# Four of the eight loads of the middle filter piece issued from GpSimd instead of SyncE

## The chip, the cores and the metric

The kernel runs on one core of a Trainium2 chip. The time is the device time of one execution in microseconds (us). TensorE does the matrix products (PE in the profile, PEld its weight loads), VectorE is DVE, ScalarE is ACT, GpSimd is POOL, SyncE is SP. SP computes nothing here; it issues DMA transfers, each of which the chip's DMA engines then carry out.

## The reference

With x of 2048 x 512 in bf16, two blocks are chained, each on a layer norm and each added to its input:

```
h  = x + irfft2( rfft2( layernorm(x) ) * (w_r + i w_i) )
h2 = h + ( gelu( layernorm(layernorm(h)).T @ w1 + b1 ) @ w2 + b2 ).T
```

The filter w_r, w_i has 2048 rows (frequencies along the sequence) and 257 columns (frequencies along the features); w1 is 2048 x 1376 and w2 is 1376 x 2048.

## The kernel before

**Stages.** The 2-D transform is done as matrix products with constant matrices. Stage A (line 593) transforms along the sequence: 16 row groups `A0` to `A15`, each four products of x with the Fourier matrix `FS`, which GpSimd scales by the rows' reciprocal deviation (`fs0` to `fs15`, line 577). Their results are copied out of PSUM as `Ye` (line 607). Then the spectrum is worked through in 16 chunks c. For each chunk: `Bc` (line 637) transforms along the features, `Bec` copies it out (line 641); `Cc` (line 652, mostly two chunks at once, named `C2p`, `C4p` and so on) finishes the sequence transform, `Cec` copies it out into `Xsb` (line 665); `Pc` (line 674, on DVE) multiplies the chunk by its part of the filter tile `W`; `Ic` (line 692) starts the inverse transform with the product as weights, and `Iec` copies its result into `TT` (lines 708 and 709). After the last chunk the inverse transform along the features (`Bi`, lines 864 and 771) and along the sequence (`Ai`) are done row group by row group, with the second layer norm (`sq`, `A2`, `hh`), and each normed row group `hh` is multiplied by w1 at once (`m1`, line 844). Then come gelu, the products with w2 (`m2`, lines 962 and 968), the final addition (`fin`, line 974) and the stores.

**Order.** Each engine runs a list of operations in a fixed order, written out by hand in `K.schedule` (line 979). What a list leaves out is placed by a small list scheduler with priorities. GpSimd's list holds the sixteen `fs`, then seven small operations `nm` (negated row means, line 617, used from the second layer norm on), three small loads of biases, and three casts of these (lines 937 to 940). SP's list is left to the scheduler: the loads go in order of `prio`. The chunk products stand in DVE's list in the order P0 P1, P3 P2, P4, P5, P7 P6, P9 P8, P10 P11, P13 P12, P14 P15, with copies out of PSUM between them.

**PSUM banks.** `I` of chunk c writes bank 5 + c % 3 (the last half of chunk 15 writes bank 0), so I14 must wait until Ie11 has copied out, and I15 until Ie12 has.

**The filter loads** (lines 510 to 523). `W` is loaded in three pieces of the index tau: 0 to 8, 8 to 18, 18 to 32. Chunk c reads tau 2c and 2c+1, so the middle piece serves P4 to P8, and the last one P9 to P15. A piece has two components, w_r and w_i, and each component four loads (six in the first piece), because a tau has four rows in four partitions. A load of the middle piece carries 32 partitions x 10 rows of 512 bytes, 160 KB; one of the last piece 14 rows, 224 KB. The source rows are 514 bytes apart.

**Waits.** All loads with one `group` share a semaphore, and whoever reads such a tile waits until all loads of the group have landed. `wgroup` only tells the dependency tracker that writes of one piece need no order among themselves. So P4 waits for all of the middle piece, and P9 for all of the last.

**After the filter** SP issues the constants `ID`, `GD` and `IF`, eight loads of w1 and eleven of w2; some of the last wait for buffers of the chunk stage to come free.

Of the kernel before, what the change touches and what calls it, by code (L numbers as in the profile page):

```python
# [11 lines left out]
NP = 128  # L12
# [453 lines left out]
def build_kernel(nc, A_x, A_w_r, A_w_i, B_w1, B_b1, B_w2, B_b2, out, verbose=False):  # L466
# [10 lines left out]
    X, Y, FS, F, E, Lm, Hm, W, TT, GD, IF = (T[n] for n in ("X", "Y", "FS", "F", "E", "Lm", "Hm", "W", "TT", "GD", "IF"))  # L477
# [9 lines left out]
    def dma(name, q, dst, src, nbytes, prio=0.0, after=(), group=None, wgroup=None, store=False, land=None):  # L487
        def emit(e, eng):
            with nc.allow_non_contiguous_dma(reason="layout"):
                return eng.dma_start(dst, src)  # L490
        return K.op(name, q, emit, ins=[src] if store else [], outs=[] if store else [dst], occ=450.0, prio=prio,
                    after=after, nbytes=nbytes, group=group, wgroup=wgroup, land=land)
# [18 lines left out]
    for pi, (ta, tb) in enumerate(pieces):  # L511
        for comp, wsrc in enumerate((A_w_r, A_w_i)):
            wv = wsrc.rearrange("(q r) k -> q r k", r=64)
            for reim in range(2):
                parts = [(0, ta, tb, wv[:, ta:tb, 1:257])]
                lo = ta
                if ta == 0:
                    parts.append((1, 0, 1, wv[:, 32:33, 1:257]))
                    lo = 1
                parts.append((1, lo, tb, wv[:, 64 - lo:64 - tb:-1, 1:257]))  # L520
                for ss, a, b, src in parts:
                    dma(f"ld_w{comp}_{pi}_{reim}_{ss}_{a}", "sp", W[2 * ss + reim:NP:4, a:b, comp, :], src, 32 * 512 * (b - a),
                        prio=1.0 + pi, group=f"W{pi}", wgroup=f"W{pi}")

    K.op("mk_eps", "dve", lambda e, eng: eng.memset(eps[:, 0:1], LN_EPS), outs=[eps[:, 0:1]], occ=70.0, lat=130.0, prio=0)  # L525
    K.op("mk_eps2", "dve", lambda e, eng: eng.memset(eps[:, 1:2], LN_EPS * LN_EPS), outs=[eps[:, 1:2]], occ=70.0, lat=130.0, prio=0)
# [21 lines left out]
    for ga, gb in RS_GROUPS:  # L548
# [18 lines left out]
        for n2 in range(ga, gb):  # L567
            if n2 < NSPLIT:
                for sg in range(2):
# [4 lines left out]
                         prio=-5 + 0.1 * g)  # L574
# [380 lines left out]
    for n2 in range(NS2):  # L955
        b = 3 + n2 % 5
# [14 lines left out]
        else:  # L971
# [19 lines left out]
               "ag14 bn15 ag15 Ye6 Ye10 Ye14 Be2 Ce0 P0 P1 Ie0_0 P3 P2 Be7 P4 Be8 P5 Ie2_0 P7 P6 Ie4_0 P9 P8 Ie6_0 P10 P11 Ie7_0 P13 P12 "  # L991
               "Ie10_0 P14 P15 Ie14_0 Ie15_0 Bie01 bq01 bq00 aq0 sd2_1 sd2_0 hh00 hh01 h01 h00 hh1 h2 sd3_0 sd3_1 sd4_0 sd4_1 h3 sd5_1 hh2 "
               "sd5_0 h4 sd6_1 sd6_0 hh3 h5 sd7_1 hh4 h6 sd8_0 sd7_0 hh5 sd8_1 h7 sd9_1 hh6 sd9_0 h8 hh7 sd10_1 sd10_0 h9 hh8".split(),
        "pool": "fs1 fs0 fs2 fs4 fs5 fs3 fs6 fs7 fs8 fs9 fs12 fs10 fs11 fs13 fs14 fs15 nm2 nm7 nm3 nm4 nm0 nm1 nm8 ld_b1a ld_b2 ld_b1b b2f "
               "b1f_a b1f_b".split(),
    })
    K.gen_sync()
# [31 lines left out]
def bass_sequential_preLN__spectral_gfnet__mixer_token_mlp__prompt_kernel(  # L1029
    nc,  # L1030
    A_x,
    A_w_r,
    A_w_i,
    B_x,
    B_w1,
    B_b1,
    B_w2,
    B_b2,
    out,
):  # L1040
    build_kernel(nc, A_x, A_w_r, A_w_i, B_w1, B_b1, B_w2, B_b2, out)
# [28 lines left out]
```

## Time and profile before

| | us |
|---|---|
| median of 4 runs | 130.95 (130.55 to 131.06) |
| the profiled execution | 130.05 |
| its span, first to last instruction | 128.2 |
| PE busy in the span | 121.2 |
| DVE busy | 65.1 |
| ACT busy | 65.1 |
| POOL busy | 12.3 |

The span is that of the profiled execution; 1.85 us of its time lie outside the span. The granted TensorE clock is 1.00 throughout. Bytes read are 20.49 MB, written 2.10 MB. A timeline line names the start, the time, the engine, the line of the code, the operation, what it writes and reads, and in brackets how long the engine sat idle before it and what released it. "SPq" rows are the issuing of transfers by SP, not the transfers. For the transfers, the profile gives the time from the issue to the landing. All loads and stores have line 490, that of the helper `dma`.

### The profile page before, as it was taken

The numbers are of one execution on the slowest core, as the hardware profiler recorded it, in microseconds if no ns is written. First come the engines' busy times: TensorE is split into PE (matmuls) and PEld (weight loads), VectorE is DVE, ScalarE is ACT, GpSimd is POOL, SyncE is SP. The second block draws the span as 40 slices with busy tenths as digits, with TensorE's granted clock in tenths as the row PEclk, the third lists the DMA queues.
The fourth block names the chain that finished last, engine by engine and source line by source line (L and its number), as shares of the span: only waits on it lengthen the run. The fifth ranks groups of instructions, "written<-read, shape, count | busy, mean of one in ns | idle before, by whom it ended". The sixth has DMA issues, their size and how long they took to land.

```text
span 128.2 us, 2045 instructions
## 1 busy us (share of the span) xinstructions
PE 121.2 (95%) x786; PEld 74.2 (58%) x786; DVE 65.1 (51%) x141; ACT 65.1 (51%) x137; POOL 12.3 (10%) x33
## 2 busy tenths in 40 slices
PE   6949979999999999999999999999999999999990
PEld 2337657777877555555444444456666666666660
DVE  1689949988978999966850000000323323324222
ACT  4789979999958999888777711222000000000000
POOL 0069980220000000000000000000000000000000
PEclk9999999999999999999999999999999999999999
DMA  3999888999999999999100000000121121121121
GB/s 101 352 389 371 239 202 196 300 342 371 387 426 419 419 416 406 245 390 392 55 0 0 0 0 5 0 0 0 41 72 51 41 80 48 41 82 41 41 84 41
DMA packets 16505, 22.71 MB, mean 177 GB/s; under 512 B 1552, under 2 KB 12304, under 8 KB 16368
## 3 DMA queue, kind: packets, MB, share of 16 engines
q1 hardware_dynamic: 15808, 21.66, 48.8%
q10 hardware_dynamic: 576, 0.92, 2.0%
q0 software_dynamic: 112, 0.01, 0.3%
q8 instruction: 6, 0.10, 0.3%
q14 instruction: 3, 0.02, 0.1%
HBM read 20.49 MB, written 2.10 MB: 176 GB/s over the span
## 4 chain that ended last, share of the span: by engine, by line
PE 90%; ACT 3%; DMA 3%; POOL 1%; DVE 1%; issue 1%
PE ps L844 29%; PE ps L962 28%; PE ps L692 6%; PE ps L637 6%; PE ps L593 5%; PE ps L771 5%; PE ps L652 3%; DMA X<-in_A_x_dram 3%; PE ps L808 2%; PE ps L968 2%; ACT Y L607 1%; ACT SQ L552 1%; PE ps L911 1%; ACT SQ L555 1%; POOL FS L577 1%; DVE OUT L974 1%
## 5 line engine op out<-in xcount | busy, mean ns | idle before, releaser
L844 PE MATMUL ps<-HH,W 128*128 128x512 bf16 (+1 forms) x170 | 39.6, 379 | 0.0
L962 PE MATMUL ps<-GT,W 128*128 128x512 bf16 (+1 forms) x165 | 35.9, 379 | 0.0
L974 DVE SCALAR_TENSOR_TENSOR OUT<-ps,B2f,H 128x512 bf16<-128x512 f32 x16 | 12.0, 751 | 46.7 <-PE ps L962 24.4
L962 PEld LDWEIGHTS ps<-GT,W 128*128 128x128 bf16 (+1 forms) x165 | 23.8, 144 | 11.9
L844 PEld LDWEIGHTS ps<-HH,W 128*128 128x128 bf16 (+1 forms) x170 | 16.9, 100 | 17.5 <-issue 0.2
L944 ACT ACTIVATE GT<-ps,B1f 128x512 bf16<-128x512 f32 (+1 forms) x11 | 7.0, 692 | 12.7 <-PE ps L844 12.7
L818 DVE TENSOR_TENSOR H<-ps,X 128x512 bf16<-128x512 f32 x14 | 9.7, 692 | 4.0 <-PE ps L808 3.4
L824 ACT ACTIVATE SQ<-H,nm 128x512 bf16<-128x512 bf16 x14 | 10.1, 722 | 2.7 <-DVE H L818 2.4
L674 DVE TENSOR_TENSOR P<-Xsb,W 128x1024 bf16<-128x1024 bf16 x16 | 10.4, 686 | 1.1 <-DMA W<-in_A_w_i_dram 1.0
L559 DVE BATCH_NORM_STATS2 st<-X 128x6 f32<-128x512 bf16 x13 | 8.3, 679 | 3.3 <-DMA X<-in_A_x_dram 3.2
L593 PE MATMUL ps<-FS,X 128*128 128x256 bf16 x64 | 7.9, 273 | 2.0 <-POOL FS L577 2.0
L781 ACT ACTIVATE EO<-ps 128x512 bf16<-128x512 f32 x15 | 8.8, 587 | 0.9 <-PE ps L771 0.7
L692 PE MATMUL ps<-Hm,P 128*128 128x128 bf16 x128 | 9.1, 220 | 0.1
L637 PE MATMUL ps<-E,Y 128*128 128x256 bf16 x64 | 8.5, 273 | 0.7 <-ACT Y L607 0.7
L771 PE MATMUL ps<-GD,TT 128*128 128x256 bf16 x60 | 9.0, 273 | 0.0
L692 PEld LDWEIGHTS ps<-Hm,P 128*128 128x128 bf16 x128 | 7.4, 98 | 1.9 <-issue 1.1
L577 POOL TENSOR_SCALAR FS<-F,rs 128x256 bf16<-128x256 bf16 x16 | 7.4, 481 | 7.5 <-ACT SQ L555 6.6
L593 PEld LDWEIGHTS ps<-FS,X 128*128 128x128 bf16 x64 | 5.4, 97 | 4.5 <-POOL FS L577 3.0
L665 ACT ACTIVATE Xsb<-ps 128x1024 bf16<-128x1024 f32 (+1 forms) x9 | 8.0, 884 | 0.0
L641 ACT ACTIVATE Bsb<-ps 128x512 bf16<-128x512 f32 x13 | 7.3, 595 | 1.2 <-PE ps L637 1.2
L771 PEld LDWEIGHTS ps<-GD,TT 128*128 128x128 bf16 x60 | 5.8, 98 | 3.0 <-ACT EO L781 0.2
L533 PE MATMUL ps<-WM 128*128 128x512 bf16 (+1 forms) x20 | 6.1, 448 | 1.2 <-DVE eps L525 1.2
(70 smaller groups left out, 97.7 us busy)
## 6 DMA issues: line engine op xcount, KB each, us to landing
W<-in_B_w_dram SPq DMA_DIRECT2D x8, 688.0 KB, 11.3
W<-in_B_w_dram SPq DMA_DIRECT2D x10, 512.0 KB, 18.2
out_dram<-OUT SPq DMA_DIRECT2D x16, 128.0 KB, 1.7
X<-in_A_x_dram SPq DMA_DIRECT2D x4, 256.0 KB, 6.3
F<-c_F SPq DMA_DIRECT2D x4, 256.0 KB, 6.2
IF<-c_IF SPq DMA_DIRECT2D x1, 1024.0 KB, 6.8
W<-in_A_w_r_dram SPq DMA_DIRECT2D x4, 224.0 KB, 3.9
W<-in_A_w_i_dram SPq DMA_DIRECT2D x4, 224.0 KB, 4.0
```

Of the source, the lines that this page charges most:

```text
L577: lambda e, eng, n2=n2: eng.tensor_scalar(FS[:, n2, :].rearrange("p (a b) -> p a b", a=2), F[:, n2 // 4, :, n2 % 4, :], rs[:, n2, 0:1], 1. ...
L593: r = eng.matmul(ps[:, b, 256 * u:256 * u + 256].rearrange("p (a b) -> p a b", a=2), X[:, n2, 128 * t:128 * t + 128], fr if t < 2 else fa, ...
L637: r = eng.matmul(o, Y[:, k, c, :], E[:, k, :].rearrange("p (h r) -> p h r", h=2), start=(i == 0), stop=(i == 3), skip_group_check=True)
L674: return eng.tensor_tensor(P[:, :, :, :], x.unsqueeze(2).broadcast_to([NP, 2, 2, 256]), W[:, 2 * c:2 * c + 2, :, :], ALU.mult)
L692: r = eng.matmul(o, P[:, h, m, par::2], Hm[:, v, m, :].rearrange("p (m r) -> p m r", r=4), start=(h == 0 and m == 0 and (par == 0 or b != ...
L771: r = eng.matmul(o, TT[:, q, n2, par, :], GD[:, par, q, :], start=(i == 0), stop=(i == 3), skip_group_check=True)
L781: return eng.activation(eo[:, :], ps[:, bE, :], ACT.Copy)
L818: K.op(f"h{n2}", "dve", lambda e, eng: eng.tensor_tensor(H[:, n2, :], ps[:, bA, :], X[:, n2, :], ALU.add), ins=[ps[:, bA, :], X[:, n2, :]] ...
L824: K.op(f"sq{n2}", "act", lambda e, eng: eng.activation(sq[:, :], hsrc, ACT.Square, bias=nm[:, n2, 0:1], accum_out=s2t[:, n2, 0:1]), ins=[h ...
L844: return eng.matmul(ps[0:Mt, bank, :], W1[:, n2, 128 * t:128 * t + Mt], HH[:, n2, :], start=(n2 == 0), stop=(n2 == 15), skip_group_check=True)
L962: r = eng.matmul(ps[:, b, :], W2[t][0:Kt, n2::16], GT[0:Kt, t, :], start=(t == 0), stop=(t == NFT - 1), skip_group_check=True)
L974: K.op(f"fin{n2}", "dve", lambda e, eng, n2=n2, b=b: eng.scalar_tensor_tensor(OUT[:, n2, :], ps[:, b, :], B2f[:, n2:n2 + 1], H[:, n2, :], ...
```

## The change

```diff
                 for ss, a, b, src in parts:
-                    dma(f"ld_w{comp}_{pi}_{reim}_{ss}_{a}", "sp", W[2 * ss + reim:NP:4, a:b, comp, :], src, 32 * 512 * (b - a),
-                        prio=1.0 + pi, group=f"W{pi}", wgroup=f"W{pi}")
+                    dma(f"ld_w{comp}_{pi}_{reim}_{ss}_{a}", "pool" if (comp, pi) == (1, 1) else "sp", W[2 * ss + reim:NP:4, a:b, comp, :], src, 32 * 512 * (b - a),
+                        prio=1.0 + pi, group=f"W{pi}{comp * (pi == 1)}", wgroup=f"W{pi}")
...
-        "pool": "fs1 fs0 fs2 fs4 fs5 fs3 fs6 fs7 fs8 fs9 fs12 fs10 fs11 fs13 fs14 fs15 nm2 nm7 nm3 nm4 nm0 nm1 nm8 ld_b1a ld_b2 ld_b1b b2f "
+        "pool": "fs1 fs0 fs2 fs4 fs5 fs3 fs6 fs7 fs8 fs9 fs12 fs10 fs11 fs13 fs14 fs15 ld_w1_1_0_0_8 ld_w1_1_0_1_8 ld_w1_1_1_0_8 ld_w1_1_1_1_8 nm2 nm7 nm3 nm4 nm0 nm1 nm8 ld_b1a ld_b2 ld_b1b b2f "
                 "b1f_a b1f_b".split(),
```

The four w_i loads of the middle piece are issued by GpSimd, after `fs15` and before the `nm`. SP issues the four w_r loads of that piece and then goes on to the last piece. The middle piece now has two semaphores, one for each component (groups `W10` and `W11`), and the readers of the piece wait for both. The first and the last piece keep one semaphore each, and nothing else changes.

## The prediction

> **What bounds the kernel now.** I read the shares of the chain that ended last first, then the list of waits, then the timelines of the engines around the filter loads.
>
> ```profile
> PE 90%; ACT 3%; DMA 3%; POOL 1%; DVE 1%; issue 1%
> ...
> DVE P L674 <- DMA W<-in_A_w_i_dram: 1.0, 1, 1.0
> ```
>
> TensorE carries the chain (90%), and from 16.74 us to the last m2 product at 125.17 it is hardly ever idle. A load shows up in one wait only behind stage A: one product P waits 1.0 us for w_i. The timeline of DVE says which:
>
> ```profile
> 23.97 0.68 DVE L674 TENSOR_TENSOR P<-Xsb,W 128x1024 bf16<-128x1024 bf16 x1
> ...
> 27.75 0.69 DVE L709 CAST TT<-ps 128x512 bf16<-128x512 f32 x1
> 29.46 0.69 DVE L674 TENSOR_TENSOR P<-Xsb,W 128x1024 bf16<-128x1024 bf16 x1 [1.02 <-DMA W<-in_A_w_i_dram]
> ```
>
> By DVE's order the product at 23.97 is P4, the first reader of the middle piece (no bracket: it did not wait), and the one at 29.46 is P9, the first reader of the last piece. Without its wait P9 starts at 29.46 - 1.02 = 28.44. SP's timeline shows why the last piece is late:
>
> ```profile
> 14.94 2.60 SPq L490 DMA_DIRECT2D W<-in_A_w_r_dram  x4
> 17.58 3.01 SPq L490 DMA_DIRECT2D W<-in_A_w_i_dram  x4
> 20.63 2.63 SPq L490 DMA_DIRECT2D W<-in_A_w_r_dram  x4
> 23.30 2.64 SPq L490 DMA_DIRECT2D W<-in_A_w_i_dram  x4
> 25.99 0.61 SPq L490 DMA_DIRECT2D ID<-c_ID  x1
> ```
>
> Rows one and two are the middle piece, three and four the last. SP issues without a break, one load per 2.67 / 4 = 0.67 us, whether of 160 or of 224 KB. The issue view, cut to single loads, gives 3.8 us from issue to landing for the last load of the middle piece (issued 19.97, so landed 23.8) and 4.1 us for the last load of the last piece (25.32, landed 29.4). So the middle piece lands 0.2 us before P4 and the last piece a full microsecond after P9 wants it. The issue rate limits, not the bytes: the windows view moves 222 GB/s in 17 to 19 us and 134 in 19 to 21, against 322 in 24 to 28.
>
> **What the change removes from SP.** The second row: 20.63 - 17.58 = 3.05 us. The last piece is issued from 17.58, its last load at 25.32 - 3.05 = 22.27, and lands at 22.27 + 4.1 = 26.4. If instead bytes limit it: both pieces are 8 x 160 KB + 8 x 224 KB = 3.15 MB; all of it from 17.0 on at 322 GB/s takes 9.8 us, to 26.8, and 0.6 us of completion gives 27.4 (the last packets of POOL's third small load are at 25.7, its landing at 26.3). Both are before 28.44, so P9's wait goes. ID, GD, IF and the w1 and w2 loads move up by the same 3.05 us at most; nobody waits for them today, so that is worth nothing.
>
> **What it adds on POOL.** Here are POOL's rows of today:
>
> ```profile
> 15.27 0.23 POOL L617 TENSOR_SCALAR nm<-mv 128x1 f32<-128x1 f32 x1
> ...
> 17.13 1.18 POOL L490 DMA_DIRECT2D B1s<-in_B_b_dram  x1
> 18.30 0.56 POOL L490 DMA_DIRECT2D B2s<-in_B_b_dram  x1
> 22.72 0.54 POOL L490 DMA_DIRECT2D B1s<-in_B_b_dram  x1 [3.85 <-DMA B1s<-in_B_b_dram]
> ```
>
> The four loads take the place of the nm at 15.27. No load of 160 KB from POOL exists, so it has bounds. *Issue:* B1s with 1280 elements of 2 bytes costs 1.18 us, B2s with 128 rows 0.56. A filter load has 320 runs, between them; by the line through the two rows it is 0.56 + 192 x 0.62 / 1152 = 0.66 us, and I take that; ends 0.54 and 1.18. So POOL is done with the four at 15.27 + 4 x 0.66 = 17.9 (17.4 to 20.0), the last being issued at 17.25 (16.9 to 18.8). *Landing:* the three small loads land 3.6, 4.3 and 5.3 us after their issue, and POOL's queue shows its first packets 2.3 us after the first issue (17.13, packets from 19.46). SP's 160 KB loads land after 3.2 to 4.4. With 2.3 us to the first packet, four loads are 655 KB from 17.6 on; at half of 322 GB/s (a choice: two queues share; the ends are all, and what SP's queue leaves) that is 4.1 us, to 21.7, plus 0.6 of completion, 22.3. With issues of 1.18 it is 18.8 + 2.3 + 160 KB at half rate (1.0) + 0.6 = 22.7, and by the slowest landing row 18.8 + 5.3 = 24.1. I take 22.3 to 22.7, ahead of P4 at 23.97. The bad end, POOL's packets served only behind SP's, is the third rival.
>
> **What waits behind these loads on POOL.** The seven nm (done by 17.19 now, by 20 to 22 then; first read by sq and hh from 40 us on), the three bias loads (the casts end at 27.12, some 3 to 5 us later then; gelu is the first reader, after 60 us). Cover of tens of microseconds: nothing. B1s's 2-byte packets meet SP's last piece instead of the gap at 19 to 21; the room from 26.4 to 28.44 pays for that. P4 gets a second wait; DVE is busy with the copy at 23.36 until then, so it is hidden.
>
> **What DVE's 1.02 us are worth.** Not 1.02. DVE is busy almost without a break from P9 to P15, but PE still has work that does not need it; what counts is the end of the stage:
>
> ```profile
> 34.78 1.58 ACT L708 ACTIVATE TT<-ps 128x512 bf16<-128x512 f32 x3
> ...
> 34.88 1.29 DVE L674 TENSOR_TENSOR P<-Xsb,W 128x1024 bf16<-128x1024 bf16 x2
> ...
> 36.35 1.03 DVE L709 CAST TT<-ps 128x512 bf16<-128x512 f32 x2 [0.19 <-PE ps L692]
> ...
> 36.95 0.38 ACT L708 ACTIVATE TT<-ps 128x256 bf16<-128x256 f32 x1 [0.59 <-PE ps L692]
> ```
>
> P14 and P15 run from 34.88 to 36.16. I14 starts 0.15 us after P14 ends (35.71 after 35.56), I15 0.15 after P15 (36.31 after 36.16); PE has gaps of 0.23 and 0.16 us between the starts there, beyond the usual 0.056 between two products. That is all that PE loses, 0.39 us. Without DVE's delay the next to be late is ACT: its timeline has no idle time from 24.68 to 36.36, so it cannot move up. Its three copies at 34.78 are Ie11, Ie12, Ie13, ending at 35.38, 35.87 and 36.36; I14 needs the bank of Ie11 and I15 that of Ie12. So I14 starts at 35.38 + 0.15 = 35.53, I15 at 36.02. DVE's Ie14 then starts at 36.17 instead of 36.35, and Ie15_0 moves with it, 0.18 us earlier; the first inverse product Bi00 (37.40) needs both. From there PE has no gap but 0.04 us, and what comes off there comes off the end. **Sum: -0.18 us**, on the profiled execution's 130.05 (span 128.2) and equally on the median, 130.95 - 0.2 = 130.75 us. The profiled execution is 0.9 us faster than the median; I can't see where, and keep that for the range.
>
> **Two rules of the Trainium skill.** Rows: in 15 to 21 us the engines move 113 to 230 GB/s of a shown 322, with SP issuing all the time. "DMA: Bandwidth & Descriptors", section Issuing engines are not separate DMA queues, says that spreading loads over engines saves only the issuing time, usually small; here that time is what limits, so row and rule part on "small", and by the rule the gain would be nothing (130.95). The same page (Queues, rings and completion order) says that a DMA engine takes its queues in turn; by that POOL's loads get their half. Against the change speaks "SBUF — State Buffer", the trap that DVE blocks DMA: POOL can't write descriptors while DVE runs in a two-port mode. The trace speaks against it here: the B1s load at 22.72 was issued beside P products and took 0.54 us, like B2s beside a copy (0.56); by the rule with its example of 3.1 us for one transfer, four would end at 15.3 + 12.4 = 27.7, an estimate of +2.7 us by the limit of 25.0 worked out under the third rival.
>
> **The rivals.**
> 1. *More than the gap of one bank.* If ACT's copies move up too, both gaps of PE vanish, -0.39; and if the 0.9 us by which the timed runs exceed the profiled one is a longer wait of P9, it goes too, up to -1.1: 129.85 to 130.5, middle 130.3. For it: an added delay of P9 passes one to one through DVE to I15. Against: no view shows the timed runs.
> 2. *A transfer that is hidden anyway, or bytes that limit.* The last piece lands no earlier because the engines are full: P9 waits as before, 130.95. Against: the 113 to 230 GB/s.
> 3. *The other side: P4 becomes the late one.* If POOL's queue gets only what SP's leaves, then SP's 2.5 MB from 17 on at 322 GB/s take until 24.7; POOL has moved some 0.2 MB in the room before 19.5 and ends its 0.4 MB at 26.0, landing at 26.6. P4 then starts 2.7 us late. Of that 1.0 is free: DVE would only reach P9 when it does today. So 26.6 - 25.0 = +1.6 to 1.7, 132.6. It decides from a landing after 25.0 us on: until there no loss, each microsecond beyond costs about one. Issues of over 1.5 us do the same. For it: no large load from POOL is in the trace. Against: B1s's 1280 elements in 1.18 us.
>
> **How the numbers follow.** Chances: forecast (-0.39 to 0) 0.55, rival 1 0.24, rival 2 0.05, rival 3 0.16. A difference under 0.3%, 0.39 us, is about what a measurement of this kernel can't tell from none. So faster 0.24, same 0.55 + 0.05 = 0.60, slower 0.16. The predicted time is 130.75. For the range I leave 0.1 out on either side: down to 130.1 (into rival 1), up to 131.9 (into rival 3, which starts at 131.3).
>
> **What would show it.** Right: the bracket of 1.02 at P9 gone, no bracket at P4, four POOL issues of about 0.66 us from 15.3 on, SP's w_r row of the last piece at 17.6, and Bi00 some 0.2 us earlier. Wrong: a wait of P4 for w_i; POOL issues over 1.2 us; P9 still waiting; Bi00 more than 0.4 us earlier or later.

## The result, and the profile after

The changed kernel takes 129.79 us in the median (43 runs, 129.33 to 130.63), the kernel before 130.8 (67 runs, 129.75 to 135.73). The ratio is 0.9945 with a 95% interval of 0.9932 to 0.9958, so the change makes the kernel 0.4 to 0.7% faster. It leaves out the longest of the runs of before, those over 1.5% above the fastest (15 of the 67; the changed kernel has none), which is why it is nearer to 1 than the two medians are. The forecast was 130.75 with a range of 130.1 to 131.9: too little by a factor of 3.6 (by the ratio) to 5 (by the medians), and outside its range. The profiled execution of the changed kernel took 129.78 us (span 128.0), only 0.27 us less than that of before (130.05), and about what was forecast. So the first question is why the timed runs gained more than the two profiles show.

The page of the changed kernel and its list of waits, the lines that answer to those of before:

```profile
PE 86%; DMA 5%; ACT 3%; DVE 2%; ACTq 1%; issue 0%; POOL 0%
...
DVE P L674 <- DMA W<-in_A_w_i_dram: 0.7, 1, 0.7
```

The wait that the change is about is still there, 0.7 us instead of 1.0. (The other shares differ because the chain now runs through another load of x at the start; stage A ends 0.08 us later than in the profile of before.) The timelines of SP, POOL and DVE in the changed kernel:

```profile
14.84 6.33 SPq L490 DMA_DIRECT2D W<-in_A_w_r_dram  x8
21.21 4.21 SPq L490 DMA_DIRECT2D W<-in_A_w_i_dram  x4
25.46 0.78 SPq L490 DMA_DIRECT2D ID<-c_ID  x1
```

```profile
15.33 2.59 POOL L490 DMA_DIRECT2D W<-in_A_w_i_dram  x4
17.95 0.25 POOL L617 TENSOR_SCALAR nm<-mv 128x1 f32<-128x1 f32 x1
...
19.82 1.01 POOL L490 DMA_DIRECT2D B1s<-in_B_b_dram  x1
```

```profile
24.05 0.68 DVE L674 TENSOR_TENSOR P<-Xsb,W 128x1024 bf16<-128x1024 bf16 x1
...
27.83 0.69 DVE L709 CAST TT<-ps 128x512 bf16<-128x512 f32 x1
29.23 1.29 DVE L674 TENSOR_TENSOR P<-Xsb,W 128x1024 bf16<-128x1024 bf16 x2 [0.71 <-DMA W<-in_A_w_i_dram]
```

POOL needs 2.59 / 4 = 0.65 us per load (0.66 was forecast), and P4 at 24.05 has no bracket. But SP's twelve remaining loads take until 25.42, where twelve at 0.67 us from 14.84 on would end at 22.9. SP is done only 0.5 us sooner than before (25.94), not 3.05. Its last load, issued at 24.19 instead of 25.32, lands at 29.1 us instead of 29.4. And yet the end of the stage moved more than the forecast had it. The inverse products I11 to I15 on PE, in the kernel before and then in the changed one:

```profile
34.13 2.79 PE L692 MATMUL ps<-Hm,P 128*128 128x128 bf16 x40
36.75 0.59 PE L533 MATMUL ps<-WM 128*128 128x512 bf16 x2
37.19 0.38 PE L857 MATMUL ps<-X,ID 128*128 128x256 bf16 x2
37.40 0.60 PE L864 MATMUL ps<-GD,TT 128*128 128x256 bf16 x4
```

```profile
34.21 2.47 PE L692 MATMUL ps<-Hm,P 128*128 128x128 bf16 x40
36.52 0.59 PE L533 MATMUL ps<-WM 128*128 128x512 bf16 x2
36.95 0.38 PE L857 MATMUL ps<-X,ID 128*128 128x256 bf16 x2
37.17 0.60 PE L864 MATMUL ps<-GD,TT 128*128 128x256 bf16 x4
```

The row of I11 to I15 shrank from 2.79 to 2.47 us, and Bi00 (line 864) comes 0.23 us earlier, 0.31 if counted from the first chunk product B0 (line 637, 16.74 before and 16.82 here).

### The profile page after: what moved, and what is told of

It is laid out like the page before. It is cut to its first block, busy times and chain, and to the rows that moved or that the text cites. A ratio compares the mean times of both kernels' runs of the same rounds, so it can differ in the third digit from the quotient of the medians.

```text
span 128.0 us, 2045 instructions
## 1 busy us (share of the span) xinstructions
PE 121.2 (95%) x786; PEld 74.1 (58%) x786; DVE 65.1 (51%) x141; ACT 65.0 (51%) x137; POOL 15.4 (12%) x37
## 4 chain that ended last, share of the span: by engine, by line
PE 86%; DMA 5%; ACT 3%; DVE 2%; ACTq 1%; issue 0%; POOL 0%
PE ps L844 29%; PE ps L962 28%; PE ps L692 6%; PE ps L637 6%; PE ps L771 5%; DMA X<-in_A_x_dram 5%; PE ps L652 3%; ACT Y L607 3%; PE ps L808 2%; PE ps L968 2%; PE ps L593 2%; PE ps L911 1%; DVE st L559 1%; ACTq L490 1%; DVE OUT L974 1%
## 5 line engine op out<-in xcount | busy, mean ns | idle before, releaser
L674 DVE TENSOR_TENSOR P<-Xsb,W 128x1024 bf16<-128x1024 bf16 x16 | 10.4, 686 | 0.8 <-DMA W<-in_A_w_i_dram 0.7
## 6 DMA issues: line engine op xcount, KB each, us to landing
out_dram<-OUT SPq DMA_DIRECT2D x16, 128.0 KB, 1.7
```

Of the source, the lines that this page charges most:

```text
L674: return eng.tensor_tensor(P[:, :, :, :], x.unsqueeze(2).broadcast_to([NP, 2, 2, 256]), W[:, 2 * c:2 * c + 2, :, :], ALU.mult)
```

## The experiments

The theories at the start: **A**, the time goes with P9's wait for the last piece, as the prediction had it, and in the timed runs that wait is longer than in the one profiled execution. **B**, in the timed runs it is P4's wait for the middle piece that costs; it landed with only 0.2 us to spare. **C**, the 1280 runs of 2 bytes of the first bias load disturb the middle piece, and the change moves them away.

### Four versions of the kernel before

The first three change one name in `emit_P`, with the condition `4 <= c <= 8`, `c >= 9` and `c >= 4`:

```diff
-        x = Xb[c // 2 % 2][:, :, c % 2, :]
+        x = Xb[c // 2 % 2][:, :, c % 2, :]; cw = c % 4 if 4 <= c <= 8 else c
...
-            return eng.tensor_tensor(P[:, :, :, :], x.unsqueeze(2).broadcast_to([NP, 2, 2, 256]), W[:, 2 * c:2 * c + 2, :, :], ALU.mult)
-        K.op(f"P{c}", "dve", m, ins=[x, W[:, 2 * c:2 * c + 2, :, :]], outs=[P[:, :, :, :]],
+            return eng.tensor_tensor(P[:, :, :, :], x.unsqueeze(2).broadcast_to([NP, 2, 2, 256]), W[:, 2 * cw:2 * cw + 2, :, :], ALU.mult)
+        K.op(f"P{c}", "dve", m, ins=[x, W[:, 2 * cw:2 * cw + 2, :, :]], outs=[P[:, :, :, :]],
```

The fourth lets the three bias loads wait for another operation:

```diff
-    dma("ld_b1a", "pool", B1s[:, 0:10], B_b1[0:1280].rearrange("(t p) -> p t", p=NP), 2560, prio=20, after=gate)
+    late = [o for o in K.ops if o.name == "Ie9_0"]; dma("ld_b1a", "pool", B1s[:, 0:10], B_b1[0:1280].rearrange("(t p) -> p t", p=NP), 2560, prio=20, after=late)
```

> The kernel before, but P4 to P8 multiply by the first piece of the filter (tau taken modulo 8), so nobody waits for the middle piece; all loads are still issued. It leaves out the use of the right filter rows in these chunks. Theory A (only P9's wait matters, as the prediction had it): no change against the kernel before, within 0.3%. Theory B (in most timed runs the middle piece lands after P4 wants it; the profiled run of before, with 0.2 us to spare, is one of the lucky ones): 0.4 to 0.8 us faster, and the spread of the single times shrinks.

> The kernel before, but P9 to P15 multiply by the first piece of the filter (tau taken modulo 8), so nobody waits for the last piece; all loads are still issued. It leaves out the use of the right filter rows in these chunks. Theory A (only P9's wait matters, and ACT caps what its loss brings in the profiled run; the timed runs have a longer wait): 0.5 to 0.9 us faster, like the change itself. Theory B (the middle piece and P4 are the larger part): 0.2 to 0.3 us faster, the spread of the single times stays.

> The kernel before, but P4 to P15 multiply by the first piece of the filter (tau taken modulo 8), so nobody waits for the middle or the last piece; all loads are still issued. It leaves out the use of the right filter rows in these chunks. Both theories: all that the two waits cost, at least 0.7 us faster than before; if it is no faster than 0.3 us, the gain of the change lies in neither wait.

> The kernel before, but the three bias loads of GpSimd wait for Ie9 (some 33 us) instead of Ye15, so that the 1280 runs of 2 bytes of the first one no longer run beside the middle piece; SP still issues all of the filter. Theory C (the gain of the change comes from moving these runs away from the middle piece): 0.4 to 0.8 us faster and less spread. Theories A and B without C: within 0.2 us of the kernel before, and the DMA engines move more than the 134 GB/s of before in 19 to 21 us only if SP's issue is not the limit there.

| version | median, us | ratio to before | 95% interval |
|---|---|---|---|
| nobody waits for the middle piece | 130.98 | 1.0021 | 0.9988 to 1.0054 |
| nobody waits for the last piece | 129.85 | 0.9943 | 0.9918 to 0.9967 |
| nobody waits for either | 129.83 | 0.9930 | 0.9902 to 0.9957 |
| bias loads later | 130.54 | 0.9977 | 0.9947 to 1.0006 |

B falls: taking P4's wait away brings nothing, although P4 does wait in some executions (0.66 us in the second profile of the kernel before, taken later). C is not supported, its interval takes in 1. One sign of C did come: with the bias loads moved away the engines moved 212 GB/s in 19 to 21 us instead of 134. So the 134, which the prediction put down to SP's issue rate alone, is probably in part the bias load; the time does not follow it. A stands: without P9's wait the kernel before is as fast as the changed one (0.9945), and without both waits not clearly faster. So the change brings all that an end of the waits for the middle and the last piece can bring.

The profile of the first version shows by accident what the first profile of before did not. SP's and DVE's timelines there:

```profile
17.52 3.56 SPq L490 DMA_DIRECT2D W<-in_A_w_i_dram  x4
21.13 2.63 SPq L490 DMA_DIRECT2D W<-in_A_w_r_dram  x4
23.80 3.39 SPq L490 DMA_DIRECT2D W<-in_A_w_i_dram  x4
```

```profile
30.96 0.69 DVE L674 TENSOR_TENSOR P<-Xsb,W 128x1024 bf16<-128x1024 bf16 x1 [2.52 <-DMA W<-in_A_w_i_dram]
```

The loads are those of the kernel before, but P9 waits 2.5 us, not 1.0. SP's rows of four loads, 2.63 us when nothing holds them up, took 3.56 and 3.39.

### What ends the stage behind the change

A1: with P9's wait short, ACT's copies end the stage, as the prediction worked out. The first version delays the bias loads of the changed kernel in the same way as above. The other two move one copy:

```diff
-               "Be0 Be1 Be3 Ce1 Be5 Be4 Ce2p Ie1_0 Be6 Ce4p Ie3_0 Be9 Ce6p Be10 Be11 Ce8p Be13 Be12 Ce10p Ie5_0 Be14 Ce12p Be15 Ie8_0 Ie9_0 "
+               "Be0 Be1 Be3 Ce1 Be5 Be4 Ce2p Ie1_0 Be6 Ce4p Ie3_0 Be9 Ce6p Be10 Be11 Ce8p Be13 Ce10p Ie5_0 Be14 Ce12p Be15 Ie8_0 Ie9_0 "
...
-               "ag14 bn15 ag15 Ye6 Ye10 Ye14 Be2 Ce0 P0 P1 Ie0_0 P3 P2 Be7 P4 Be8 P5 Ie2_0 P7 P6 Ie4_0 P9 P8 Ie6_0 P10 P11 Ie7_0 P13 P12 "
+               "ag14 bn15 ag15 Ye6 Ye10 Ye14 Be2 Ce0 P0 P1 Ie0_0 P3 P2 Be7 P4 Be8 P5 Ie2_0 P7 P6 Ie4_0 Be12 P9 P8 Ie6_0 P10 P11 Ie7_0 P13 P12 "
```

> The changed kernel, but the three bias loads of GpSimd wait for Ie9 instead of Ye15, so the 1280 runs of 2 bytes no longer meet the last filter piece. Theory A1 (behind the change ACT's copies end the stage, and a wait of P9 up to some 0.7 us is free): P9's wait in the profile shrinks below 0.4 us, and the time stays within 0.15 us of the changed kernel, 0.6 to 0.85 us under the kernel before. Rival (what is left of P9's wait still costs): 0.3 to 0.7 us faster than the changed kernel.

> The changed kernel, with the copy Be12 taken from ACT to DVE, between Ie4 and P9, where DVE sits idle for P9's load. Theory A1 (behind the change ACT's copies end the stage): 0.15 to 0.35 us faster than the changed kernel, 0.85 to 1.1 us under the kernel before. Rival (P9's wait or PE itself ends the stage): within 0.1 us of the changed kernel.

> The kernel before, with the copy Be12 taken from ACT to DVE, between Ie4 and P9. Theory A1 (in the kernel before P9's wait on DVE ends the stage in most timed runs, not ACT): within 0.2 us of the kernel before. Rival (ACT ends the stage there too): 0.2 to 0.4 us faster.

Changed kernel with late bias loads: 129.73 us, ratio to before 0.9938 (0.9915 to 0.9962). Changed kernel with Be12 on DVE: 129.86, 0.9936 (0.9917 to 0.9956). Kernel before with Be12 on DVE: 130.62, 0.9990 (0.9963 to 1.0016). Neither of the first two beats the changed kernel (0.9945) by more than its interval. In the first, P9's wait is gone altogether. PE, DVE and ACT there:

```profile
34.09 2.43 PE L692 MATMUL ps<-Hm,P 128*128 128x128 bf16 x40
36.35 0.59 PE L533 MATMUL ps<-WM 128*128 128x512 bf16 x2
36.79 0.38 PE L857 MATMUL ps<-X,ID 128*128 128x256 bf16 x2
37.01 0.60 PE L864 MATMUL ps<-GD,TT 128*128 128x256 bf16 x4
```

```profile
27.71 0.69 DVE L709 CAST TT<-ps 128x512 bf16<-128x512 f32 x1
28.32 1.28 DVE L674 TENSOR_TENSOR P<-Xsb,W 128x1024 bf16<-128x1024 bf16 x2
...
36.09 1.02 DVE L709 CAST TT<-ps 128x512 bf16<-128x512 f32 x2 [0.33 <-PE ps L692]
```

```profile
34.75 1.57 ACT L708 ACTIVATE TT<-ps 128x512 bf16<-128x512 f32 x3
36.55 0.39 ACT L708 ACTIVATE TT<-ps 128x256 bf16<-128x256 f32 x1 [0.23 <-PE ps L692]
```

Both gaps of PE are gone: 39 steps of 0.056 us and 0.22 for the last product make 2.40. ACT's list is the same as before and its copies Ie11 and Ie12 end at 35.35 and 35.84; I14 and I15 start at 35.44 and 35.91, I14 without any gap and I15 0.02 us late. From 16.7 to 37.0 us PE is busy all the time. So ACT was not what stood behind P9's wait, or for 0.02 us at most; PE's own work is. A1 falls in this, while its number for this version (P9's wait is free, no gain) came out. The changed kernel with Be12 on DVE does not test ACT cleanly. ACT is relieved there and sits idle for 0.45 and 0.28 us in the stage, but P9 now starts at 29.50 behind the added copy, and Bi00 follows 7.92 us later: DVE took up what ACT gave. On the kernel before, the same move changes nothing (0.9990), as A1 and the long wait of P9 both have it.

### What holds SP up

In the profile of before, the one filter load that SP takes long to issue (1.03 us, within the row 17.58 3.01) starts 0.25 us after a 16 KB transfer on the instruction queue. Theory F says that such transfers, TensorE's code, hold it up. The test:

```diff
-    emit_warm("s", 16, 6, -1)
+    emit_warm("s", 64, 6, -1, w=128)
```

> The kernel before, with 64 warming products of 128 columns at the start instead of 16 of 512: the same columns, 96 more TensorE instructions ahead of stage A. Theory F (SP's long issue at 18.9 us is held up by a 16 KB transfer of the instruction queue, which brings TensorE's code each time it has gone through some 240 instructions): that transfer comes some 8 us earlier, near 10 us, the next one near 24 us, and SP's long issues of over 0.9 us move with both; the load row around 18 us has none. Rival G (SP is held up by what it loads itself, or by the bias load): the long issue stays at 18 to 20 us.

One run, 130.96 us beside 130.67 for the kernel before. The queue lines of the DMA view say where the transfer is; it is listed in 18.6 to 19.6 us in the profile of before and in 13.1 to 14.0 and 26.6 to 27.5 in this one (each time one packet of 0.02 MB), at 18.7, 13.1 and 26.6 to the tenth. SP's timeline in this version:

```profile
6.74 4.11 SPq L490 DMA_DIRECT2D W<-in_A_w_r_dram  x6
10.89 4.14 SPq L490 DMA_DIRECT2D W<-in_A_w_i_dram  x6
15.07 2.60 SPq L490 DMA_DIRECT2D W<-in_A_w_r_dram  x4
17.71 2.60 SPq L490 DMA_DIRECT2D W<-in_A_w_i_dram  x4
...
26.85 1.03 SPq L490 DMA_DIRECT2D IF<-c_IF  x1
```

The row at 17.7, which holds a lengthened issue (0.77 to 2.29 us instead of 0.62) in every other profile with the old order, has none (2.60); the long issues are now at 13.5 (0.89 us) and at 26.85 (1.03 against 0.43), each within 0.4 us of the moved transfer. F stands in direction, and rival G falls for this issue; the places were off by some 3 us, and no run shows why. All fourteen profiles agree with F: the filter load that SP issues beside the first such transfer of the chunk stage (in this version the one at 13.1) takes 0.77 to 2.29 us. But P9 waited here too, 2.16 us, with SP done earlier than in the profile of before: the last load took 5.3 us from issue to landing instead of 4.1. A transfer of this queue lies between the two in both profiles, so it does not explain the difference. Other long issues have no such transfer beside them (1.38 us at 25.8 in the version without P4's wait, 0.98 at 21.8 in the next section's first, 1.42 at 21.2 and 1.22 at 24.2 in the changed kernel), so code is one cause and not the only one.

### SP's relief alone, and more executions of both kernels

The first version leaves out the four loads altogether; the others are the two kernels, unchanged:

```diff
-                for ss, a, b, src in parts:
+                for ss, a, b, src in (() if (comp, pi) == (1, 1) else parts):
```

> The kernel before, without the four w_i loads of the middle piece on any engine; P4 to P8 multiply by the first piece of the filter instead (tau taken modulo 8). It leaves out these 0.66 MB and the use of the right filter rows in these chunks. So SP is relieved as in the change, but POOL issues nothing more. Theory D (the last piece's landing sets the time until TensorE's own work does; SP's relief is what the change brings): the last piece lands some 2.7 us earlier than in the kernel before, at 26.7 to 28.2 us, P9 doesn't wait, and the time is that of the changed kernel, 0.6 to 0.9 us under the kernel before. Rival H (POOL's earlier or parallel loading brings the gain): within 0.3 us of the kernel before.

> The kernel before, unchanged, for one more profile. Theory D (the five profiles with SP's loads in the old order all have Bi00 8.0 us after the last piece's landing and the span's end 98.8 us after it, and the landing varies from 29.4 to 30.9): landing between 29.4 and 31 us, a wait of P9 of 1.0 to 2.5 us, Bi00 at landing + 8.0, span = landing + 98.8. Rival I (the other versions had long waits because of their edits, the kernel before always waits 1.0 us): a wait of 0.9 to 1.1 us, span 128.2.

> As before_again, one more execution of the kernel before, unchanged: by theory D a landing that differs from the first profile's by some tenths of a microsecond or more, Bi00 at landing + 8.0, span = landing + 98.8; by rival I a wait of 0.9 to 1.1 us.

> The changed kernel, unchanged, for one more profile. Theory D (its landing is early enough that TensorE's own work sets Bi00, 20.3 us after the first chunk product B0, or nearly so): landing at 28.4 to 29.3 us, Bi00 20.3 to 20.5 us after B0, span 127.6 to 128.4.

Beside 131.08 us for the kernel before on the same chip: SP's relief alone 129.84, ratio 0.9894 (0.9849 to 0.9938); the changed kernel 129.91, 0.9908 (0.9875 to 0.9941); the kernel before once more 130.67, 0.9969 (0.9933 to 1.0005), and its third profile 130.61 in one run. So taking the four loads off SP is enough for the whole gain, and rival H falls. This version also moves 0.66 MB less, so it does not tell SP's issuing from the bytes; the changed kernel, which moves them all, gains as much. The last piece lands at 27.0 us here. SP's timeline with the four loads left out, and DVE's:

```profile
14.61 5.77 SPq L490 DMA_DIRECT2D W<-in_A_w_r_dram  x8
20.43 3.00 SPq L490 DMA_DIRECT2D W<-in_A_w_i_dram  x4
```

```profile
28.15 1.28 DVE L674 TENSOR_TENSOR P<-Xsb,W 128x1024 bf16<-128x1024 bf16 x2
```

SP needs 8.8 us for the twelve loads, 1.8 us less than in the changed kernel (14.84 to 25.42; 1.6 less than in its second profile). That is about what POOL's 655 KB cost SP; it is not seen in the time, because in both versions PE's own work is what ends last, or nearly so.

Rival I falls as well. The kernel before has three profiles now, the DVE rows of P9 in the second and the third:

```profile
31.13 1.29 DVE L674 TENSOR_TENSOR P<-Xsb,W 128x1024 bf16<-128x1024 bf16 x2 [1.84 <-ACT TT L708]
```

```profile
30.06 1.29 DVE L674 TENSOR_TENSOR P<-Xsb,W 128x1024 bf16<-128x1024 bf16 x2 [1.50 <-DMA W<-in_A_w_i_dram]
```

In the second the bracket names ACT's copy into TT, which P9 neither reads nor writes; the last w_i load, issued at 26.48, lands at 31.0: it is the load again. The load is late for two reasons. In the second profile SP issues it late (26.48 instead of 25.32). In the third it is issued a little earlier than in the first (25.15), but takes 4.8 us to land instead of 4.1. All fourteen profiles together, read from the timelines (B0 and Bi00 on PE, P9 on DVE):

| profile | P9's wait | P9 starts | Bi00 | Bi00 - P9 | Bi00 - B0 | span |
|---|---|---|---|---|---|---|
| before, first | 1.02 | 29.46 | 37.40 | 7.94 | 20.66 | 128.2 |
| before, Be12 on DVE | 0.81 | 29.95 | 37.89 | 7.94 | 21.32 | 128.7 |
| before, third | 1.50 | 30.06 | 37.99 | 7.93 | 21.13 | 128.8 |
| before, late bias | 1.76 | 30.41 | 38.35 | 7.94 | 21.40 | 129.2 |
| before, longer warming | 2.16 | 30.41 | 38.34 | 7.93 | 21.79 | 129.2 |
| before, no wait for the middle piece | 2.52 | 30.96 | 38.90 | 7.94 | 22.16 | 129.7 |
| before, second | 1.84 | 31.13 | 39.06 | 7.93 | 22.04 | 129.9 |
| before, no wait for the last piece | none | 29.28 | 37.45 | 8.17 | 20.39 | 128.3 |
| before, no wait for either | none | 28.80 | 37.48 | 8.68 | 20.30 | 128.3 |
| after, first | 0.71 | 29.23 | 37.17 | 7.94 | 20.35 | 128.0 |
| after, second | 0.50 | 29.29 | 37.39 | 8.10 | 20.30 | 128.2 |
| after, Be12 on DVE | none | 29.50 | 37.42 | 7.92 | 20.42 | 128.2 |
| after, late bias | none | 28.32 | 37.01 | 8.69 | 20.31 | 127.8 |
| SP's relief alone | none | 28.15 | 36.83 | 8.68 | 20.30 | 127.6 |

This is theory D: Bi00 comes 7.94 us after P9 or 20.30 us after B0, whichever is later, and the span ends 90.8 us after Bi00. The 20.30 is the floor, the time that PE's own work takes. The two numbers are read from these profiles, but were on record (as 8.0 behind the landing, and 20.3) before the last four of them were taken: both kernels' second ones, the third of before and SP's relief alone. The rule holds to 0.02 us in thirteen of the fourteen; without the wait for the last piece, where P4 waits 0.69 us, Bi00 is 0.09 later. In the nine profiles with SP's loads in the old order the last piece lands between 29.4 and 31.3 us, in the changed kernel's two at 29.1 and 29.2.

## Why the prediction was wrong

**The step that failed first: the wait of P9 was taken from one execution and given "equally" to the median.** The profiled execution had 1.02 us, near the shortest of what the loads of before do; the other profiles have up to 2.52. That the two first profiles differ by 0.27 us, about the forecast, is luck: P9 still waits 0.71 us in the changed one, and the terms below were wrong. The numbers to see it were there: the profiled execution was 0.9 us under the median, and below each of the four timed runs shown. The rival that read this as a longer wait (rival 1, given 0.24) was the right one, and the objection to it, that no view shows the timed runs, was no evidence against it. With the table the medians can be worked back to the wait, as an estimate: 130.8 us is a span of 130.8 - 1.85 = 128.95, so Bi00 at 38.15 and P9 at 30.2; the changed kernel's 129.79 is Bi00 at 37.14, the floor for a B0 at 16.84. P9 would be ready 11.70 us after B0 (28.44 - 16.74), at 28.54, so the typical wait of before is some 1.7 us. Of this 20.30 - 7.94 - 11.70 = 0.66 is free, and 1.0 shows: the difference of the medians.

**SP's row of 3.05 us** was taken as a fixed saving. Four such loads take 2.60 us when nothing holds them up; the other 0.4 was a hold-up that grew to 1.7 in other executions (the row of four took 2.77 to 4.27 us, 2.60 in the version with longer warming). The time from the last load's issue to its landing varies as well, from 4.1 to 5.3 us. What the change gives is a reserve against both, not a fixed 3 us.

**The term of the sum, -0.18 us,** was mis-sized: 20.66 - 20.30 = 0.36 was to be had on the profiled execution, and the changed kernel's profile shows 0.31 of it. Two errors. The step from the end of ACT's copy to the product that reuses its bank was given the 0.15 us that lie between P's end and I14 or I15; in the profile without P9's wait I14 and I15 start 0.09 and 0.07 us after Ie11 and Ie12 end, with a gap of 0.02 on PE in all. And Bi00 was said to need both copies of chunk 15: by line 866 it reads the half that ACT copies (Ie15_1); DVE's half, which was to be the limit, runs until 37.11 in the profile with late bias loads, while Bi00 starts at 37.01. "The next to be late is ACT" was wrong, it is PE.

**"So P9's wait goes"** was wrong: the last piece did not land at 26.4 to 27.4 but after 29. The bound by bytes took 322 GB/s with SP issuing freely; with two queues SP was held up for 2.5 us in its twelve loads. Part of the delay is the bias load, for which the prediction set aside the room up to 28.44: in the profile with that load moved away the last piece lands at 28.2, 0.9 us earlier. By the free 0.66 us the wait that was left cost 0.05 us in the first profile and nothing in the second.

**Right were** POOL's issue time, the landing before P4 (the last of the four loads at 22.9, 22.3 to 22.7 forecast), that nothing behind the loads on POOL matters, and that a late P4 is cheap: where P9 to P15 read other data, P4 waited 0.69 us in the profile and Bi00 came 20.39 us after B0, 0.09 over the floor. The rule of the Trainium skill from "DMA: Bandwidth & Descriptors", section Issuing engines are not separate DMA queues, that more issuing engines save only issue time, agrees with the runs: leaving the loads out of SP's list without any other engine issuing them gave the same gain. Its "usually small" does not fit here: the issue of a load takes 0.67 us, its bytes at the 322 GB/s of the profile 0.51 to 0.71. Of the trap in "SBUF — State Buffer", that DVE blocks POOL's descriptors, there is no sign in the four issues of 0.59 to 0.81 us; whether DVE was in the mode that the trap needs, no run here tells.

**What stays open:** why SP's issue beside one 16 KB transfer takes anything from 0.8 to 2.3 us, what held SP up where there was none, and why the last load takes from 4.1 to 5.3 us to land.

## What to carry to other kernels

A wait for a transfer that shows in one profile is a sample; when the timed runs lie above the profiled one, profile again before pricing it, and read where its landing comes from (a queue that is issued without a break passes every hold-up on). Work out the free part of a wait from the next bound with the waits of its own instructions, product by product: two gaps of 0.2 us decided here. And look at the spread: taking loads off a queue that issues without a break narrowed it here, the middle half of the runs lies within 1.0 us before and 0.36 us after.

## What the runs showed of the hardware

- Transfers of code stand beside held-up issuing of loads: a 16 KB packet of the instruction queue came in the chunk stage (at 18.7 and 28.5 us in the profile of before), the first moved to 13.1 us when 96 instructions were put in TensorE's program, and the filter load that SP issued beside it took 0.8 to 2.3 us instead of 0.62, 0.89 at the new place.
- Loads that POOL issues slow down SP's issuing: with POOL's 655 KB beside them SP's twelve loads from 14.8 on took 10.6 us (9.8 to 10.4 in the three other profiles), without them 8.8.
- A load of 1280 runs of 2 bytes is dear while the engines are full: in the changed kernel the bytes moved fall to 216 and 239 GB/s in 23 to 25 us, from 340 the microsecond before, and with that load moved away they are 345 and 304. In the second profile the fall is to 173, in 24 to 25 us.
